# Block kinds from a written table, two more factor sets, and split weights for all columns of the last batch

## The chip, the cores and the metric

The kernel runs on one core of a Trainium2 chip. Its time is the device time of one execution in microseconds (us). Before the change it was 1623.45 us, the median of 4 runs (1623.39 to 1623.63).

The core has five engines with a queue each, worked off in the order in which the program puts instructions there: PE (TensorE, matrix products, with its weight loads shown as PEld), DVE (VectorE), ACT (ScalarE), POOL (GpSimd) and SP (SyncE, which here only issues DMAs). An engine waits at an instruction until the instructions on other engines that it depends on are done.

## What is computed

An attention block with learned inducing points, and then a gated feed-forward block without bias, in 32-bit floats:

```python
def mab(q, kv):
    s = scale * (q @ kv.transpose(0, 2, 1))
    a = softmax(s)                     # written out as max, exp, sum
    return a @ kv
h = mab(I, x)                          # x: 4 batches of 12416 rows, 128 channels; I: 32 rows
x = mab(x, h).reshape(49664, 128)
xn = x / sqrt(mean(x * x) + 1e-6) * rms_g
g = xn @ w_gate                        # 128 -> 1536
out = (silu(g) * (xn @ w_val)) @ w_out # 1536 -> 128
```

The feed-forward block is nearly all of the work: for each row, two products of 128 by 1536 and one of 1536 by 128.

## The kernel before

**Batches, units, blocks.** The four batches are worked off one after the other. The rows of a batch form 25 units: 20 of 512 rows, 4 of 480 and 1 of 256 (line 96). The 1536 hidden columns form NJ = 12 blocks of 128. So a batch has 300 blocks and the whole run 1200; one block of one unit is a *slot* (`slot`, line 674).

**What a slot does.** PE makes the gate product g (line 677) into one of five PSUM banks, ACT takes its SiLU (685), PE makes the value product v (688) into another bank, and DVE multiplies the two (694). The result t, 128 hidden columns by up to 512 rows, must then be multiplied by 128 rows of w_out and added into the unit's accumulator `acc`. There are three ways, the *kinds* of a block:

- *plain*: t goes to SBUF as `u`, and PE multiplies it by the 32-bit `wo` (613 with `acc<-u,wo` in the profile). The profile shows such a product as two records on PE.
- *sums*: t stays in its PSUM bank; ACT makes a rounded, scaled part `hi` of it (659), DVE the remainder `lo` and with it frees the bank (660), and POOL the factor `d` = hi - lo (669).
- *differences*: t goes to SBUF; ACT makes the rounded part (663), POOL the remainder (664), ACT the scaled `hi` (668), and POOL the factor `d` (669).

A block of either of the last two kinds is called *split* here. PE then makes three products in the faster 32-bit type (`F32R`) in place of the plain one: `hi` and `lo` with two parts of the weights into a bank `u3` (633, 635), and `d` with a third part into `acc` (613 with `acc<-xn,more`). When a unit's last split block is through, ACT copies `u3` out (638); `finish` adds it to `acc` (621), transposes and stores.

**Factor sets.** The three factors of a block lie in one of RING = 4 sets, which are taken round-robin from three buffers of `xn` (569 to 571). A set is busy from the first factor until the three products are issued. The three parts of w_out exist for blocks 0 to 9 only (NK = 10, `split_wo`, 566; `weight_of`, 596): blocks 10 and 11 of every unit are plain.

**Stacks.** The weights of g and v differ by batch (they are folded with the inducing rows) and lie in the tiles `sg` and `sv`, two buffers each. Those of the next batch are placed by DMA from its block 199 on (`place`, 459), the tiles being taken at block 193 (`square_h`). Until then the other buffer of each is idle.

**The order.** Attention work for the next batch, and the normalisation (`seam`, 483), is strewn between slots by block number (`schedule`, 823). Which kind a block has, and when PE does the waiting last products, is settled before the program is written, by `rehearse` (929): it runs through all slots with fixed durations for each engine, and records for each slot which products PE does ahead of g, ahead of v and ahead of each step (`picks`). The kind is picked there, slot by slot, by `decide` (1051): sums if that fits, else differences if that fits, else plain. `fits` (1037) adds the candidate's load to eight slots of each engine's load and refuses it where an engine would fall behind PE by more than

```python
LIMIT = (0, 0.8, 0.8, 2.6)   # us: PE, DVE, ACT, POOL (line 926)
```

or by 0.25 us more than it would without. `decide` also refuses blocks near the switches of ACT's table for the exponentials, the first units, and blocks beyond the seventh of the very last unit. Of the 1200 blocks 495 come out plain, 566 sums and 139 differences.

Of the kernel before, what the change touches and what calls it, by code (L numbers as in the profile page):

```python
# [23 lines left out]
def kernel(  # L24
# [74 lines left out]
    NK = NJ - 2  # L99
    RING, RESERVE, HELD, SILU = 4, 7, 9, 3  # L100

    def pool(name, bufs, **kw):
# [463 lines left out]
    def split_wo(step):  # L566

        if not step:
            kws["first"] = xnp.tile([P, half + NK, C], F32R, name=f"xn{full - 1}")
            for name in ("hi", "lo", "d"):  # L570
                kws[name] = xnp.tile([P, RING, 512], F32R, name=f"xn{full - 4 + len(kws) - 2}")

# [9 lines left out]
        for g in range(2):  # L582
# [10 lines left out]
            if at == 6:  # L593
                scaled(0, g, 4096.0)

    def weight_of(kind, j):
        n = kind * NK + j
        return kws["first"][:, n, :] if n < half + NK else kws["more"][:, n - half - NK, :]

    def ffn(b, u):  # L600
# [27 lines left out]

        def project3(j, hi, lo, d):
            if st["k"] == nk:  # L630
                st["u"] = ps_u.tile([P, 512], F32, name="u3")
            ups = st["u"]
            nc.tensor.matmul(ups[:, 0:T], weight_of(0, j), hi, start=st["k"] == nk, stop=False)  # L633
            st["k"] -= 1
            nc.tensor.matmul(ups[:, 0:T], weight_of(1, j), lo, start=False, stop=not st["k"])  # L635
            if not st["k"]:
                o = st["o"] = outp.tile([P, 512], F32, name="o")
                nc.scalar.activation(o[:, 0:T], ups[:, 0:T], AF.Copy, scale=1.0 + 2.0 ** -12)
            project(weight_of(2, j), d)
            kws["out"] -= 1  # L640

# [9 lines left out]
        def three(j, t):  # L651

            assert kws.get("out", 0) < RING
            kws["out"] = kws.get("out", 0) + 1
            n = kws["n"] = (kws.get("n", 0) + 1) % RING
            hi, lo, d = (kws[name][:, n, 0:T] for name in ("hi", "lo", "d"))
            v, kind = t[:, 0:T], kinds[b, u, j]
# [8 lines left out]
            def rest():  # L666
                if kind != "sums":
                    nc.scalar.activation(hi, d.bitcast(F32), AF.Copy, scale=2.0 ** -12)
                nc.gpsimd.tensor_tensor(out=d, in0=hi.bitcast(F32), in1=lo.bitcast(F32), op=ALU.subtract)  # L669
                kara.append(lambda: project3(j, hi, lo, d))  # L670

# [127 lines left out]
    if B > 1:  # L799
        for _ in range(R):  # L800
            load_channels(*pieces[1].pop(0))

    COST = {"turn_x": (0, .63), "scores1": (1.07, .7), "max1": (0, .1), "max2": (.13, .85), "max3": (.1, .1), "turn_e": (0, .63),
            "exp1_of": (0, 0, 1.14), "sum_h": (1.85, .25), "fold_l": (.06, .15), "divide": (0, .6), "turn_h": (.2, .8),
            "square_h": (.1, .76), "stack": (1.1, 1.32), "scores2": (1.07, .63), "row_max": (0, .59), "sub_max": (0, 0, 0, 1.01),
            "exp2": (0, 0, 1.0), "turn_a": (0, .63), "square": (.87,), "turn_z": (0, 1.23), "scale": (0, .7),
            "root": (0, 0, 0, 2.9), "apply": (0, 0, 0, 1.01), "turn_b": (0, .63), "split": (0, 0, .51, 1.25),
            "power": (0, .45), "power_number": (0, 0, .63), "upper": (0, .6), "upper_number": (0, 0, .53), "sign": (0, .6),
            "lower": (0, .6, 0, 1.26), "stack_of": (.87, 0, .5), "stack_low": (0, .62), "split_wo": (0, 0, .7, 1.52)}
    BANKS = {"scores1", "sum_h", "max2", "max3", "fold_l", "turn_h", "square_h", "stack", "scores2", "square", "stack_of"}  # L810
# [3 lines left out]
    TAIL = {"PE": .17, "DVE": .09, "ACT": .11, "POOL": .04}  # L814
    MADE = {"sums": ((-.16,), (0, .6, .49), (0, 0, 0, 1.25)), "differences": ((-.16,), (0, 0, .53, 1.25), (0, 0, .52, 1.25))}
    loads = [[1.29, .6, .5, 0.0] for k in range(B * NU * NJ + 24)]

    def load(k, *costs, sign=1):
        for i, one in enumerate(costs):
            for e, us in enumerate(one):  # L820
                loads[k + i][e] += sign * us

    def schedule(b):
# [4 lines left out]
        def add(k, step, *args):  # L828
            plan.setdefault(int(k), []).append((step, args))
            load(b * NU * NJ + int(k), COST.get(step.__name__, ()))  # L830

        def exponentials(k, step, first):

            groups = list(range(first, NS - 1, 2))
            for i, s in enumerate(groups):
                add(k + i, step, s, NS if s == groups[-1] else s + 2)
                if i:
                    by_tanh.add((b, k + i))
            for at in (k, k + len(groups)):
                load(b * NU * NJ + at, (0, 0, 1.3))  # L840
            return k

        if not b:
# [10 lines left out]
            for s in range(1, NS):  # L854
                add(2 * s + 16, f["scores2"], s)
                add(2 * s + 17, f["row_max"], s)
                add(2 * s + 18, f["sub_max"], s)
            marks.append(exponentials(3 * NS + 9, f["exp2"], 1))
        if b + 1 < B:
            g = attention(b + 1, b + 2 < B)  # L860
# [33 lines left out]
    for k, (b, s) in enumerate(order):  # L894
# [5 lines left out]
        for late_by, one in enumerate(following):  # L900
            for i, step in enumerate(seam(*one)):
# [3 lines left out]
                seams.setdefault(at, []).append((step, ()))  # L905
                load((b * NU + at[1]) * NJ + j, COST.get(step.__name__, ()))
    by_tanh = set()
# [17 lines left out]

    LIMIT = (0, 0.8, 0.8, 2.6)
    kinds, picks = {}, {}

    def rehearse():
# [5 lines left out]
        queues, uses, later, left = {"plain": [], "three": []}, [0], [], {}  # L935
        split = {"out": 0, "u3": 0.0, "all": 0, "made": 0}

# [7 lines left out]
        def soon(k, step):  # L945
            later.append([k, step])

        def has(kind, by):
            if not queues[kind]:
                return False  # L950
            t, unit = queues[kind][0][:2]
            if kind == "three" and not left[unit]["three"]:
                t = max(t, split["u3"])
            return t <= by
# [4 lines left out]
        def issue(kind, to):  # L959
            to.append(kind)  # L960
            t, unit, w = queues[kind].pop(0)[:3]
            split["all"] -= 1
            st = left[unit]
            if kind == "plain":
                end = run("PE", 0.858 * w, t)
            else:
                end = run("PE", 0.697 * w, t)
                split["out"] -= 1
                split["made"] -= 1
                st["three"] += 1  # L970
# [12 lines left out]
        def close(unit, w):  # L983
            st = left[unit]

            def finish():
                run("DVE", 0.6 * w, st["end"], st.get("u3", 0.0))
                soon(1, lambda: run("DVE", 0.63 * w))

# [46 lines left out]

        def fits(k, kind, behind):

            def ahead():
                now = list(behind)  # L1040
                for i in range(k, k + 8):
                    now = [max(0.0, x + one - loads[i][0]) for x, one in zip(now, loads[i])]
                    yield list(now)

            before = list(ahead())
            load(k, *MADE[kind])
            if all(x <= max(most, y + 0.25) for now, old in zip(ahead(), before) for x, y, most in zip(now, old, LIMIT)):
                return True
            load(k, *MADE[kind], sign=-1)

        def decide(b, k, u, j):
            n = b * NU * NJ + k
            if (j >= NK or b == 0 and (u < 2 or k < 26) or (b, u) == flat[-1] and j > 6 or split["out"] > RING or
                    near(b, k, -3, 2)):
                return None
            s = at["PE"]
            behind = [0.0] + [max(0.0, at[e] - s - off) for e, off in (("DVE", 1.2), ("ACT", 0.45), ("POOL", 1.45))]
            return next((kind for kind in ("sums", "differences") if fits(n, kind, behind)), None)

        def slot(b, k, u, j, tanh):  # L1060
            w = per2[units[u][0]] * m / 512.0
            st = left.setdefault((b, u), dict(left=NJ, three=0, open=0, all=False, slots=0, end=0.0))
            kind = decide(b, k, u, j)
            first, second = [], []
# [11 lines left out]
            if kind != "sums":  # L1076
                uses[0] += 1
                while queues["plain"] and queues["plain"][0][3] <= uses[0] - HELD:
                    issue("plain", second)
            while split["made"] == RING and any(one[0] == 1 and one[1].__name__ == "three" for one in later):  # L1080
                issue("three", second)
# [18 lines left out]
            if kind:  # L1100
                kinds[b, u, j] = kind
                split["out"] += 1
                st["open"] += 1

                def three():
                    split["made"] += 1
                    hi = run("ACT", (0.49 if kind == "sums" else 0.53) * w, t)
# [5 lines left out]
                    def rest():  # L1113
                        h = hi if kind == "sums" else run("ACT", 0.52 * w, hi)
                        d = run("POOL", 1.25 * w, lo, h)
                        queues["three"].append((d + 0.05, (b, u), w))

# [20 lines left out]
    for b in range(B):  # L1138
        plan, marks = plans[b]

        unit = {}
        for k, (u, j) in slots(b):

            def steps():
# [54 lines left out]
```

## Time and profile before

| | |
|---|---|
| median of 4 runs | 1623.45 us |
| the profiled execution, its own time | 1623.39 us |
| its span, first to last instruction | 1621.6 us |
| ahead of the first slot's g product | 55.3 us |
| PE busy | 1604.1 us, 99% |
| DVE busy | 1444.5 us, 89% |
| ACT busy | 1238.3 us, 76% |
| POOL busy | 1217.7 us, 75% |

The profile is of one execution. Busy time is the union of an engine's instruction spans. Matmuls are pipelined and their ends are modelled, so that a busy PE is not yet a PE at its peak: what a slot costs PE is better read from the starts of successive products in the timeline. An instruction's span on DVE and ACT is also longer than the distance to the next one's start when they follow without a gap: 128x512 products on DVE last 0.67 us on the mean and start 0.60 us apart; on ACT 0.60 and 0.49; on POOL 1.29 and 1.25.

### The profile page before, as it was taken

The numbers are of one execution on the slowest core, as the hardware profiler recorded it, in microseconds if no ns is written. First come the engines' busy times: TensorE is split into PE (matmuls) and PEld (weight loads), VectorE is DVE, ScalarE is ACT, GpSimd is POOL, SyncE is SP. The second block draws the span as 40 slices with busy tenths as digits, with TensorE's granted clock in tenths as the row PEclk, the third lists the DMA queues.
The fourth block names the chain that finished last, engine by engine and source line by source line (L and its number), as shares of the span: only waits on it lengthen the run. The fifth ranks groups of instructions, "written<-read, shape, count | busy, mean of one in ns | idle before, by whom it ended". The sixth has DMA issues, their size and how long they took to land.

```text
span 1621.6 us, 25435 instructions
## 1 busy us (share of the span) xinstructions
PE 1604.1 (99%) x7085; PEld 1085.1 (67%) x7085; DVE 1444.5 (89%) x2504; ACT 1238.3 (76%) x2285; POOL 1217.7 (75%) x979
## 2 busy tenths in 40 slices
PE   8999999999999999999999999999999999999998
PEld 6546666756676666766677666676667777777776
DVE  4879988999899998899899998789989999999997
ACT  4667877767887778776777777877778888878886
POOL 1358885878588886688678888587858878878876
PEclk9999999999999999999999999999999999999999
DMA  7455624344363141634445323353221122111221
GB/s 262 91 72 85 114 41 100 86 97 69 60 94 59 36 95 29 133 78 79 70 66 83 55 55 67 64 124 79 46 38 29 31 39 40 35 35 36 40 38 26
DMA packets 389181, 112.52 MB, mean 69 GB/s; under 512 B 365072, under 2 KB 369712, under 8 KB 386480
## 3 DMA queue, kind: packets, MB, share of 16 engines
q1 hardware_dynamic: 388304, 110.82, 34.9%
q8 instruction: 56, 0.92, 0.2%
q14 instruction: 85, 0.70, 0.1%
q10 hardware_dynamic: 736, 0.08, 0.0%
HBM read 53.95 MB, written 27.00 MB: 50 GB/s over the span
## 4 chain that ended last, share of the span: by engine, by line
PE 94%; DVE 1%; ACT 1%; issue 1%; POOL 0%; DVEq 0%; ACTq 0%
PE acc L613 35%; PE gv L677 18%; PE gv L688 16%; PE u L635 10%; PE u L633 10%; PE gv L322 3%; PE gv L499 1%; PE gv L378 1%; DVE gv L694 1%; ACT silu L685 1%; PE gv L453 0%; DVE xn L660 0%; PE gv L467 0%; DVE o L621 0%; POOL xn L279 0%
## 5 line engine op out<-in xcount | busy, mean ns | idle before, releaser
L669 POOL TENSOR_TENSOR xn<-xn,xn 128x512 fp32r<-128x512 f32 (+2 forms) x705 | 870.8, 1255 | 268.5 <-DVE xn L660 158.6
L685 ACT ACTIVATE silu<-gv 128x512 f32<-128x512 f32 (+2 forms) x1186 | 689.7, 586 | 258.3 <-PE gv L677 231.5
L688 PE MATMUL gv<-a,sv 128*128 128x512 f32 (+2 forms) x1188 | 636.0, 535 | 0.9 <-ACT silu L685 0.8
L613 PE MATMUL acc<-u,wo 128*128 128x512 f32 (+1 forms) x990 | 490.8, 580 | 0.0
L677 PE MATMUL gv<-a,sg 128*128 128x512 f32 (+2 forms) x1188 | 486.7, 410 | 1.5 <-ACT silu L685 0.8
L694 DVE TENSOR_TENSOR u<-silu,gv 128x512 f32<-128x512 f32 (+2 forms) x621 | 407.6, 663 | 51.7 <-PE gv L688 32.5
L694 DVE TENSOR_TENSOR gv<-silu,gv 128x512 f32<-128x512 f32 (+2 forms) x565 | 376.0, 668 | 66.2 <-PE gv L688 49.0
L660 DVE SCALAR_TENSOR_TENSOR xn<-xn,gv 128x512 fp32r<-128x512 f32 (+2 forms) x566 | 371.2, 656 | 9.5 <-ACT xn L659 5.9
L659 ACT ACTIVATE xn<-gv 128x512 fp32r<-128x512 f32 (+2 forms) x566 | 330.4, 584 | 43.2 <-DVE gv L694 30.9
L677 PEld LDWEIGHTS gv<-a,sg 128*128 128x128 f32 x1188 | 223.7, 188 | 189.4 <-ACT silu L685 40.1
L688 PEld LDWEIGHTS gv<-a,sv 128*128 128x128 f32 x1188 | 223.5, 188 | 139.7 <-issue 45.9
L613 PE MATMUL acc<-xn,more 128*128 128x512 f32 (+2 forms) x705 | 273.5, 388 | 3.0 <-DVE o L621 2.7
L633 PE MATMUL u<-xn,xn 128*128 128x512 f32 (+2 forms) x705 | 272.3, 386 | 0.0
L613 PEld LDWEIGHTS acc<-u,wo 128*128 128x128 f32 x990 | 184.9, 188 | 46.8 <-issue 9.1
L664 POOL TENSOR_TENSOR xn<-u,xn 128x512 fp32r<-128x512 f32 (+2 forms) x139 | 178.6, 1285 | 41.6 <-ACT xn L663 41.6
L635 PE MATMUL u<-xn,xn 128*128 128x512 f32 (+2 forms) x414 | 160.0, 387 | 0.0
L613 PEld LDWEIGHTS acc<-xn,more 128*128 128x128 f32 x705 | 132.3, 188 | 33.5 <-POOL xn L669 5.7
L633 PEld LDWEIGHTS u<-xn,xn 128*128 128x128 f32 x705 | 132.5, 188 | 28.6 <-issue 5.5
L663 ACT ACTIVATE xn<-u 128x512 fp32r<-128x512 f32 (+2 forms) x139 | 87.4, 629 | 36.7 <-DVE u L694 32.4
L635 PE MATMUL u<-xn,more 128*128 128x512 f32 (+2 forms) x291 | 112.5, 387 | 0.0
L516 POOL TENSOR_TENSOR rs<-ms,mhalf 128x16 f32<-128x16 f32 (+2 forms) x28 | 75.9, 2710 | 18.2 <-DVE ms L511 17.2
L635 PEld LDWEIGHTS u<-xn,xn 128*128 128x128 f32 x414 | 77.7, 188 | 17.5 <-DVE gv L694 0.2
(151 smaller groups left out, 1096.4 us busy)
## 6 DMA issues: line engine op xcount, KB each, us to landing
out_dram<-o SPq DMA_DIRECT2D x320, 64.0 KB, 2.0
xT<-in_x_dram SPq DMA_DIRECT2D x60, 256.0 KB, 5.1
xn<-in_x_dram SPq DMA_DIRECT2D x60, 256.0 KB, 4.9
a<-hi SPq DMA_DIRECT2D x156, 64.0 KB, 2.0
a<-lo SPq DMA_DIRECT2D x156, 64.0 KB, 2.0
xn<-in_x_dram SPq DMA_DIRECT2D x5, 1024.0 KB, 10.0
xn<-w SPq DMA_DIRECT2D x18, 256.0 KB, 3.2
out_dram<-o SPq DMA_DIRECT2D x64, 60.0 KB, 2.0
```

Of the source, the lines that this page charges most:

```text
L613: nc.tensor.matmul(acc[:, 0:T], lhsT, rhs, start=st["left"] == NJ, stop=st["left"] == 1)
L633: nc.tensor.matmul(ups[:, 0:T], weight_of(0, j), hi, start=st["k"] == nk, stop=False)
L635: nc.tensor.matmul(ups[:, 0:T], weight_of(1, j), lo, start=False, stop=not st["k"])
L659: nc.scalar.activation(hi, v, AF.Copy, scale=(1.0 - 2.0 ** -13) * 2.0 ** -12)
L660: nc.vector.scalar_tensor_tensor(out=lo, in0=hi.bitcast(F32), scalar=-4096.0, in1=v, op0=ALU.mult, op1=ALU.add)
L663: nc.scalar.activation(d, v, AF.Copy, scale=1.0 - 2.0 ** -13)
L664: nc.gpsimd.tensor_tensor(out=lo, in0=v, in1=d.bitcast(F32), op=ALU.subtract)
L669: nc.gpsimd.tensor_tensor(out=d, in0=hi.bitcast(F32), in1=lo.bitcast(F32), op=ALU.subtract)
L677: nc.tensor.matmul(g[:, 0:T], sg[:, ts(j, P)], a[:, 0:T], start=True, stop=True)
L685: nc.scalar.activation(sl[:, 0:T], g[:, 0:T], AF.Silu)
L688: nc.tensor.matmul(v[:, 0:T], sv[:, ts(j, P)], a[:, 0:T], start=True, stop=True)
L694: nc.vector.tensor_tensor(out=t[:, 0:T], in0=sl[:, 0:T], in1=v[:, 0:T], op=ALU.mult)
```

## The change

- **Kinds from a table.** `decide`, `fits`, LIMIT, MADE and the bookkeeping of loads go. The kinds stand in the program as 900 letters (`s` sums, `d` differences, `.` plain): 300 for batch 0, 300 for batches 1 and 2, 300 for batch 3. `rehearse` still settles the order of the products on PE.
- **Two more factor sets.** The two free buffers of `sg` and `sv` are lent as sets 4 and 5, each with its three factors in thirds of the tile: from block 20 of batch 0 and block 2 of the others. From block 184 they are taken back (`leaving`) except in the last batch, and must be back at block 192. Sets are now taken from a list of idle ones.
- **Split weights for blocks 10 and 11 in the last batch.** `split_last` makes their three parts in the free buffer `xT0` at blocks 2, 4 and 6 of batch 3, with three instructions on ACT and two on POOL of 128x256.
- **In the rehearsal** some PE costs of attention steps are 0.1 to 0.15 us higher, the first product of a unit waits until its bank of `acc` is free (`bank_of`), and the sets are counted as above.

The kinds come out as 411 plain, 561 sums and 228 differences; 34 of the split ones are blocks 10 and 11 of the last batch. In numbers by width, before to after:

| | 512 rows | 480 rows | 256 rows |
|---|---|---|---|
| plain | 393 to 323 | 87 to 78 | 15 to 10 |
| sums | 438 to 446 | 96 to 87 | 32 to 28 |
| differences | 129 to 191 | 9 to 27 | 1 to 10 |

505 of the 1200 blocks change their kind. The number of DMAs is the same.

```diff
+    LENT = (RING, RING + 1)
...
         if not step:
             kws["first"] = xnp.tile([P, half + NK, C], F32R, name=f"xn{full - 1}")
-            for name in ("hi", "lo", "d"):
-                kws[name] = xnp.tile([P, RING, 512], F32R, name=f"xn{full - 4 + len(kws) - 2}")
+            rings = [xnp.tile([P, RING, 512], F32R, name=f"xn{full - 4 + n}") for n in range(3)]
+            kws["sets"] = [[ring[:, n, :] for ring in rings] for n in range(RING)]
+            idle.extend(range(RING))
...
+    def lend(b, k, idle, leaving):
+        if k == (20 if not b else 2):
+            idle += LENT
+            return True
+        if b + 1 < B and k == 184:
+            leaving += [n for n in LENT if n not in idle]
+            idle[:] = [n for n in idle if n not in LENT]
+        assert k != 192 or not leaving
+
+    def give_back(n, idle, leaving):
+        leaving.remove(n) if n in leaving else idle.append(n)
+
+    def lend_tiles():
+        tiles = [stk.tile([P, F], F32R, name=name) for name in ("sg", "sv")]
+        kws["sets"][RING:] = [[t[:, ts(n, 512)] for n in range(3)] for t in tiles]
+
+    def split_last(step):
+        n = NJ - NK
+        if not step:
+            kws["last"] = xtp.tile([P, 3 * n, C], F32R, name="xT0")
+        one, (whi, wlo, ws) = wo[:, NK:NJ, :], (kws["last"][:, ts(kind, n), :] for kind in range(3))
+        if step == 0:
+            nc.scalar.activation(whi, one, AF.Copy, scale=1.0 - 2.0 ** -13)
+            nc.gpsimd.tensor_tensor(out=wlo, in0=one, in1=whi.bitcast(F32), op=ALU.subtract)
+        if step == 1:
+            nc.scalar.activation(wlo, wlo.bitcast(F32), AF.Copy, scale=4096.0)
+            nc.gpsimd.tensor_tensor(out=ws, in0=wlo.bitcast(F32), in1=whi.bitcast(F32), op=ALU.subtract)
+        if step == 2:
+            nc.scalar.activation(whi, whi.bitcast(F32), AF.Copy, scale=4096.0)
+
     def weight_of(kind, j):
+        if j >= NK:
+            return kws["last"][:, kind * (NJ - NK) + j - NK, :]
...
-        def project3(j, hi, lo, d):
+        def project3(j, where):
+            hi, lo, d = (one[:, 0:T] for one in kws["sets"][where])
...
-            kws["out"] -= 1
+            give_back(where, idle, leaving)
...
-            assert kws.get("out", 0) < RING
-            kws["out"] = kws.get("out", 0) + 1
-            n = kws["n"] = (kws.get("n", 0) + 1) % RING
-            hi, lo, d = (kws[name][:, n, 0:T] for name in ("hi", "lo", "d"))
+            where = idle.pop(0)
+            hi, lo, d = (one[:, 0:T] for one in kws["sets"][where])
...
+        if b + 1 == B:
+            for step in range(3):
+                add(2 + 2 * step, split_last, step)
...
-    LIMIT = (0, 0.8, 0.8, 2.6)
+    letters = """
+        ..........................dd...dsd...d....dssd..dssdss.ssd..sdd.sdd.dd...ss.ssd.ss...dsdsdd.s...sssd
...
+        ..sssssss.dsds.s..ssss.ds.sssdds...ssss.ssssssdsss..sdsssd...s..sss.s..dsssdd.ds...dsssssssd.sd.dd..
+    """
+    BLOCKS = [letters[NU * NJ * n:NU * NJ * (n + 1)] for n in (0, 1, 1, 2)]
...
+        def bank_of(unit):
+            older = flat.index(unit) - 2
+            if older < 0 or flat[older] not in left:
+                return 0.0
+            return left[flat[older]].get("turned", 1e9)
...
-            kind = decide(b, k, u, j)
+            kind = {"s": "sums", "d": "differences"}.get(BLOCKS[b][k])
...
-            while split["made"] == RING and any(one[0] == 1 and one[1].__name__ == "three" for one in later):
+            while not idle and any(one[0] == 1 and one[1].__name__ == "three" for one in later):
                 issue("three", second)
```

## The prediction

> **What bounds the kernel now.** I read the page first (shares of busy time, the chain), then PE's timeline for the price of a slot, then the groups by shape, the waits, and busy time by stretch.
>
> ```profile
> span 1621.6 us, 25435 instructions
> ...
> PE 1604.1 (99%) x7085; PEld 1085.1 (67%) x7085; DVE 1444.5 (89%) x2504; ACT 1238.3 (76%) x2285; POOL 1217.7 (75%) x979
> ...
> PEclk9999999999999999999999999999999999999999
> ...
> PE 94%; DVE 1%; ACT 1%; issue 1%; POOL 0%; DVEq 0%; ACTq 0%
> PE acc L613 35%; PE gv L677 18%; PE gv L688 16%; PE u L635 10%; PE u L633 10%; PE gv L322 3%; PE gv L499 1%; PE gv L378 1%; DVE gv L694 1%; ACT silu L685 1%; PE gv L453 0%; DVE xn L660 0%; PE gv L467 0%; DVE o L621 0%; POOL xn L279 0%
> ```
>
> PE bounds it: 94% of the chain that ended last is PE, at a granted clock in the top tenth throughout. Busy PE is partly modelled, so the price of a slot comes from the starts. PE's timeline, columns start and length:
>
> ```profile
> 900.31 0.40 PE L677 MATMUL gv<-a,sg 128*128 128x512 f32 x1
> 900.54 0.39 PE L633 MATMUL u<-xn,xn 128*128 128x512 f32 x1
> 900.77 0.40 PE L635 MATMUL u<-xn,more 128*128 128x512 f32 x1
> 901.01 0.39 PE L613 MATMUL acc<-xn,more 128*128 128x512 f32 x1
> 901.24 0.39 PE L688 MATMUL gv<-a,sv 128*128 128x512 f32 x1
> 901.47 0.39 PE L677 MATMUL gv<-a,sg 128*128 128x512 f32 x1
> 901.70 1.02 PE L613 MATMUL acc<-u,wo 128*128 128x512 f32 x2
> 902.15 0.80 PE L688 MATMUL gv<-a,sv 128*128 128x512 f32 x1
> 902.79 0.39 PE L677 MATMUL gv<-a,sg 128*128 128x512 f32 x1
> ```
>
> From one gate product to the next, the slot with the three products of a split block takes 901.47 - 900.31 = 1.16 us, the one with a plain product 902.79 - 901.47 = 1.32 us. Nothing waits in either. Over the run the medians are 1.160 (498 such slots) and 1.323 (295).
>
> Groups by shape (instructions | busy, mean ns | idle before, what ended it), a wait of PE, and two stretches of 100 us (PE, PEld, DVE, ACT, POOL busy):
>
> ```profile
> L669 POOL TENSOR_TENSOR xn<-xn,xn 128x512 fp32r<-128x512 f32 x567 | 720.7, 1291 | 192.1 <-DVE xn L660 103.5 <-PE gv L677 34.3 <-PE acc L613 18.1
> L664 POOL TENSOR_TENSOR xn<-u,xn 128x512 fp32r<-128x512 f32 x129 | 166.8, 1293 | 41.6 <-ACT xn L663 41.6
> L613 PEld LDWEIGHTS acc<-xn,more 128*128 128x128 f32 x705 | 132.3, 188 | 33.5 <-POOL xn L669 5.7 <-issue 0.5
> ...
> PE acc L613 <- DVE o L621: 2.7, 3, 0.9
> ...
> 1000.00:1100.00 100.00, 99.78 (x538) 67.29 (x537) 84.35 (x146) 76.57 (x138) 70.58 (x54) 1.00 0.37 81
> 1300.00:1400.00 100.00, 99.89 (x381) 71.27 (x380) 91.94 (x150) 79.13 (x146) 82.21 (x63) 1.00 0.18 34
> ```
>
> A split block costs POOL 1.29 us (sums) or 2.58 us (differences). PE's last product of it has waited for POOL's factor only 5.7 us in the whole run. POOL's share differs by stage, 71% to 82% here, and PE is no idler where it is higher.
>
> **The change, part by part.**
>
> *Kinds.* 84 more blocks are split (plain 495 to 411; 70 of 512 rows, 9 of 480, 5 of 256). At 512 rows each saves PE 1.323 - 1.160 = 0.163 us. At 480 the tail of the timeline has 1.09 (1581.38 to 1582.47) against 1.24 (1584.66 to 1585.90): 0.15. At 256 no pure plain slot stands; half of the 512 price, 0.08, is an estimate. 70 x 0.163 + 9 x 0.15 + 5 x 0.08 = 11.4 + 1.4 + 0.4 = **13.2 us off PE**, the engine on the path. The two blocks 10 and 11 per unit of the last batch are 34 of these 84.
>
> *What pays for it.* Sums go down by 5, differences up by 89. POOL gets 89 more remainders and 84 more factors: by width 132 x 1.291 + 27 x 1.22 + 14 x 0.738 = 214 us. ACT gets 8 x 0.60 - 9 x 0.57 - 4 x 0.38 for sums and 62 x 1.26 + 18 x 1.20 + 9 x 0.80 for differences: 105 us. DVE loses 2 us. Shares become POOL 1432/1610 = 89%, ACT 1343/1610 = 83%, DVE 90%. None of it lies on PE; the cover is PE's own 1.16 us or more per slot, and it holds as long as no engine is past it for longer than the factor sets bridge.
>
> *By stage.* I took each stretch of 50 blocks of the run before, and added the change of kinds at the distances between starts (POOL 1.25 us, ACT 0.49 to 0.54, DVE 0.60). Batch 2, blocks 200 to 249 (1121.5 to 1192.7): plain 18 to 13, differences 5 to 9, sums 27 to 28; POOL 58.8 + 9 x 1.25 = 70.1 of 71.2 - 0.8 = 70.4 us, 99%; DVE 94%, ACT 79%. The highest shares of POOL that come out: 99% there in the first three batches, 95% at blocks 150 to 199, and in the last batch 98%, 96% and 100% at blocks 100 to 249 in a row. Before, no such stretch has POOL above 88%. So POOL is filled nearly to PE's time, and not over it.
>
> *How far POOL falls behind in between.* A running sum, block by block, of POOL's work (the two instructions, and the attention steps) less the slot's PE time, never below zero: before, the mean is 0.6 us and the peak 2.9; after, the mean is 2.0 and the peaks 4 to 6, with 8.6 once, at blocks 100 to 125 of batch 0. This is the wait that can take the place of the saving: PE's order is fixed, so behind a product whose `d` is late stand all later g and v, and behind them SiLU and DVE. The bounds: the 5.7 us that PE waited for `d` may grow with the mean backlog, 2.0/0.6 = 3.3 times, to 19 (+13); or this wait and that for the bank of `acc` (2.7 us, which the rehearsal now counts) vanish: -8.4. Six sets bridge some six slots, 7 us, four sets 4.6 us; all peaks but two or three lie under that, and the row nearest to the new state, the stretch from 1300, shows no idle PE at POOL 82%. I take -1, the `acc` wait partly gone.
>
> *DVE beside a busier POOL.* By the trace's instructions, the DVE multiply of a slot (128x512) takes 681 ns where POOL works beside it for over 95% of its length (593 of them) and 683 ns where it hardly does (84): no price. The Trainium skill, "SBUF — State Buffer", section "Who interferes with whom", says that DVE and GpSimd share one port pair under an exclusive lock, on which the second one blocks. Read as holding for every instruction it speaks against this change: 214 us more of POOL would push DVE, at 89%, past PE. The same section frees a DVE instruction with at most one SBUF input outside the two-port modes; the slot's multiplies read one operand from PSUM, and the two durations agree. By the first reading the sum would end far slower, by the second it stays as it is.
>
> *Lent sets.* Their first writer in a batch waits for the last g and v of the batch before, done two blocks earlier. Taken back late they would hold up `place`, whose stacks are needed some 100 slots later: hidden by over 100 us. Their DMAs and those queued behind on SP are the same in number. Priced at 0; without that cover it is the length of the delay, a few us per batch.
>
> *`split_last`.* Three ACT instructions of 0.38 and two POOL of 0.74 (the rows of 256 columns), 2.6 us, off PE, at blocks where POOL's share comes to 90%. First needed at block 11: 0.
>
> *The end.* Before, PE's last products are plain; after, three split blocks stand last, two of the three differences, so POOL's chain sets the end. In the last unit POOL gets some 6.3 us for blocks 3 to 9 (at 0.70), PE has about 5.6: at worst +3, and -2 if the 2.0 us which PE loses there now (0.6, 1.1, 0.3 at slots 293, 294, 296) go. I take +1, nearer to the new chain.
>
> **Sum.** -13.2 - 1 + 1 = -13.2 against the profiled 1623.39 us (span 1621.6 and 1.8 around it, 0.06 below the median): 1610.2. As the term for late factors is one-sided in risk, I round up to **1611 us**.
>
> **The rivals.**
>
> *A. It gives nearly all back (same, 1616 to 1627).* Late `d`s cost PE up to the +13 worked out above: 1610.2 + 14 = 1624. For it: the backlog is three times as long. Against: extra sets, and an order on PE that was laid out for these kinds.
>
> *B. POOL becomes the bound (slower).* The place is blocks 200 to 249 of the first three batches and 100 to 249 of the last. If POOL can in practice be kept busy for no more than a share c of a stretch, each stretch lasts its POOL work divided by c. Over all stretches this adds 10 us at c = 0.96, 15 at 0.95, 22 at 0.94, 39 at 0.92. It decides from c = 0.955 down: at 0.94 the time is 1610 + 22 = 1632, at 0.92 1649. For it: 0.88 is the most that the run before shows, and each POOL instruction waits for others. Against: within runs POOL goes without gaps (four factors in 5.04 us at 988.73), at a spread of 1.248 median to 1.259 for nine in ten.
>
> *C. It gives more.* Waits of 0.15 to 0.6 us in some 30 slots before sum to about 10 us; kinds chosen over a whole run may avoid them too: 1600 to 1606. Against: shares that high leave less play.
>
> *D. The change doesn't do what it says:* the lent sets stay unused or the letters don't take. The built program's instruction list excludes it: 411 plain, and `sg`, `sv` as factors.
>
> **How the numbers follow.** Forecast (1606 to 1616) 0.52; C (below 1606) 0.18; A 0.17, of which 0.07 below 1620.2 and 0.10 within 0.2%; B 0.13. A measurement of this kernel tells about 0.2%, 3.2 us, from no change: faster means below 1620.2, slower above 1626.7. Faster 0.52 + 0.18 + 0.07 = 0.77, same 0.10, slower 0.13. The range leaves out B, the upper part of A and the lowest part of C (some 0.04): 1601 to 1622.
>
> **What would show it.** In the profile after: 323 plain products of 512 rows (646 records); the slots' 1.16 and 1.32 us unchanged; POOL near 89%; the multiply on DVE still near 0.68 us; PE's waits for POOL's factor at 5 to 10 us in all. A figure over 15 there, with the highest 50-block stretches longer than before, is A or B. Wrong, too, if POOL's instructions grow longer, or if the end after the last g takes over 3 us more than now.

## The result, and the profile after

The changed kernel takes **1621.32 us** (median of 42 runs, 1620.37 to 1622.21), the kernel before 1623.04 us on the same chips (60 runs, 1622.21 to 1623.84). The ratio is 0.9989, with a 95% interval of 0.9984 to 0.9993: a gain of 1.7 us, a tenth of a per cent, where 12.4 were forecast. The profiled execution took 1621.94 us.

The page of the kernel after, beginning with its span, then the busy time of each engine, the granted clock, and the shares of the chain that ended last:

```profile
span 1620.0 us, 26069 instructions
...
PE 1594.7 (98%) x7169; PEld 1098.7 (68%) x7169; DVE 1454.6 (90%) x2499; ACT 1304.4 (81%) x2461; POOL 1427.0 (88%) x1154
...
PEclk9999999999999999999999999999999999999999
...
PE 86%; ACT 3%; DVE 3%; issue 2%; POOL 2%; DMA 1%; SPq 1%; POOLq 0%; DVEq 0%; ACTq 0%
```

The shares of the loads came out near the forecast: POOL 88%, ACT 81%, DVE 90%. But DVE, which was to lose 2 us of work, is busy 10.1 us more (1444.5 to 1454.6). PE is busy 9.4 us less, yet the span is only 1.6 us shorter, and PE's share of the chain has dropped from 94% to 86%: other engines now hold it up here and there. The same two stretches of 100 us as before (PE, PEld, DVE, ACT, POOL busy):

```profile
1000.00:1100.00 100.00, 99.27 (x550) 69.11 (x549) 87.42 (x150) 83.04 (x153) 92.30 (x71) 1.00 0.38 82
1300.00:1400.00 100.00, 99.39 (x391) 72.30 (x390) 95.80 (x156) 84.75 (x159) 94.32 (x74) 1.00 0.17 32
```

PE is short of full by 0.73 and 0.61 us in 100, against 0.22 and 0.11 before; DVE went up by 3 to 4 points in both. Which waits these are, PE's waits say (us in total, times, longest):

```profile
PE gv L716 <- ACT silu L724: 4.4, 8, 1.0
PE gv L716 <- DVE u L733: 3.3, 6, 1.5
PE gv L727 <- DVE u L733: 2.4, 5, 1.2
...
PE acc L653 <- POOL xn L708: 0.4, 1, 0.4
```

At its products PE waits for POOL's factor hardly at all. It waits with the next g or v, because DVE's product (`u`) or ACT's SiLU, which free a PSUM bank, are late. Before, the two waits for `u` were not in the list, and the one for SiLU at the g product was

```profile
PE gv L677 <- ACT silu L685: 1.3, 2, 0.8
```

**Where the span went.** I fitted one price per kind of PE instruction to the distances between starts in both traces where nothing waits, summed them over all PE instructions from the first g product to the last to get *PE's work*, and call what the distances have above it *stall*. The fit is an estimate; the slots' medians, 1.160 and 1.323 us, are the same in both traces.

| us | before | after | change | forecast |
|---|---|---|---|---|
| ahead of the first g | 55.3 | 54.9 | -0.4 | 0 |
| PE's work | 1513.1 | 1499.7 | -13.4 | -13.2 |
| stall | 45.8 | 55.7 | +9.9 | -1 |
| after the last g product | 7.3 | 9.7 | +2.4 | +1 |
| span | 1621.6 | 1620.0 | -1.6 | -13.2 |

So the saving is there in full, and 12.3 us of it are given back. By stretches of 100 blocks the stall grew in the first three batches nearly everywhere, by up to 4.3 us at blocks 200 to 299 of batch 0 (4.25 to 8.56), and fell at the end of the last (3.79 to 1.67).

**What is late on DVE.** Groups of DVE by shape (instructions | busy, mean ns | idle before). In the kernel before, the scaling of the sums of squares in `scale`:

```profile
L511 DVE TENSOR_SCALAR ms<-ms 128x16 f32<-128x16 f32 x20 | 6.4, 318 | 0.7
L511 DVE TENSOR_SCALAR ms<-ms 128x15 f32<-128x15 f32 x4 | 2.3, 573 | 0.1
L511 DVE TENSOR_SCALAR ms<-ms 32x8 f32<-32x8 f32 x4 | 0.6, 158 | 0.1
```

In the kernel after:

```profile
L512 DVE TENSOR_SCALAR ms<-ms 128x16 f32<-128x16 f32 x20 | 15.8, 792 | 0.7
L512 DVE TENSOR_SCALAR ms<-ms 32x8 f32<-32x8 f32 x4 | 2.4, 606 | 0.1
L512 DVE TENSOR_SCALAR ms<-ms 128x15 f32<-128x15 f32 x4 | 2.2, 540 | 0.1
```

The same instruction on the same 16 numbers per partition has become 2.5 times as long. Over its three shapes and 28 instructions it took 9.3 us of DVE before and takes 20.4 us after. The timeline shows what it is waiting out (start, length, idle before in brackets):

```profile
112.65 0.67 DVE L511 TENSOR_REDUCE ms<-z 128x16 f32<-128x512 f32 x1
113.01 1.27 POOL L708 TENSOR_TENSOR sg<-sg 128x512 fp32r<-128x512 f32 x1
...
113.35 0.96 DVE L512 TENSOR_SCALAR ms<-ms 128x16 f32<-128x16 f32 x1
114.23 1.27 DVE L733 TENSOR_TENSOR u<-silu,gv 128x512 f32<-128x512 f32 x2
114.39 2.91 POOL L517 TENSOR_TENSOR rs<-ms,mhalf 128x16 f32<-128x16 f32 x1
114.96 0.50 PE L716 MATMUL gv<-a,sg 128*128 128x512 f32 x1 [1.45 <-DVE u L733]
```

POOL's factor runs to 113.01 + 1.27 = 114.28, the scaling to 113.35 + 0.96 = 114.31. The products behind it on DVE start late, their banks come free late, and PE stands 1.45 us. This is the rule of all of them: in the two traces together 36 of the 56 scalings have a POOL instruction in progress at their start (9 of 28 before, 27 of 28 after), and each of the 36 ends 20 to 36 ns after an instruction of POOL ends. For 34 it is the one that was in progress, and the scaling takes at most 1.17 us; two, of 1.31 and 2.02 us, end only with POOL's next instruction. The other 20 take 158 to 176 ns.

### The profile page after: what moved, and what is told of

Its sections match the earlier page's. It is cut to its first block, busy times and chain, and to the rows that moved or that the text cites. A ratio compares the mean times of both kernels' runs of the same rounds, so it can differ in the third digit from the quotient of the medians.

```text
span 1620.0 us, 26069 instructions
## 1 busy us (share of the span) xinstructions
PE 1594.7 (98%) x7169; PEld 1098.7 (68%) x7169; DVE 1454.6 (90%) x2499; ACT 1304.4 (81%) x2461; POOL 1427.0 (88%) x1154
## 4 chain that ended last, share of the span: by engine, by line
PE 86%; ACT 3%; DVE 3%; issue 2%; POOL 2%; DMA 1%; SPq 1%; POOLq 0%; DVEq 0%; ACTq 0%
PE acc L653 29%; PE gv L716 17%; PE gv L727 15%; PE u L676 10%; PE u L674 10%; PE gv L323 2%; PE gv L379 1%; PE gv L500 1%; ACT silu L724 1%; DVE u L733 1%; POOL xn L708 1%; ACT sc L440 0%; ACT xn L698 0%; DVE gv L733 0%; DVE xn L699 0%
## 5 line engine op out<-in xcount | busy, mean ns | idle before, releaser
L708 POOL TENSOR_TENSOR xn<-xn,xn 128x512 fp32r<-128x512 f32 (+2 forms) x605 | 746.2, 1252 | 78.3 <-DVE xn L699 34.4
L653 PE MATMUL acc<-u,wo 128*128 128x512 f32 (+2 forms) x822 | 409.7, 581 | 0.6 <-DVE u L733 0.6
L698 ACT ACTIVATE xn<-gv 128x512 fp32r<-128x512 f32 (+2 forms) x433 | 252.5, 583 | 65.8 <-DVE gv L733 53.5
L699 DVE SCALAR_TENSOR_TENSOR xn<-xn,gv 128x512 fp32r<-128x512 f32 (+2 forms) x433 | 283.7, 655 | 12.7 <-ACT xn L698 7.0
L703 POOL TENSOR_TENSOR xn<-u,xn 128x512 fp32r<-128x512 f32 (+2 forms) x172 | 217.4, 1264 | 13.2 <-ACT xn L702 13.2
L674 PE MATMUL u<-xn,xn 128*128 128x512 f32 (+2 forms) x581 | 228.7, 394 | 0.0
L653 PE MATMUL acc<-xn,more 128*128 128x512 f32 (+2 forms) x581 | 224.5, 386 | 0.6 <-POOL xn L708 0.4
L708 POOL TENSOR_TENSOR sv<-sv 128x512 fp32r<-128x512 f32 (+2 forms) x92 | 117.8, 1280 | 10.2 <-DVE sv L699 5.6
L674 PEld LDWEIGHTS u<-xn,xn 128*128 128x128 f32 x581 | 109.3, 188 | 25.1 <-issue 5.6
L708 POOL TENSOR_TENSOR sg<-sg 128x512 fp32r<-128x512 f32 (+1 forms) x92 | 118.1, 1284 | 7.0 <-PE u L676 2.0
L676 PE MATMUL u<-xn,xn 128*128 128x512 f32 (+2 forms) x288 | 110.7, 384 | 0.0
```

Source lines behind the costliest of these rows:

```text
L653: nc.tensor.matmul(acc[:, 0:T], lhsT, rhs, start=st["left"] == NJ, stop=st["left"] == 1)
L698: nc.scalar.activation(hi, v, AF.Copy, scale=(1.0 - 2.0 ** -13) * 2.0 ** -12)
L699: nc.vector.scalar_tensor_tensor(out=lo, in0=hi.bitcast(F32), scalar=-4096.0, in1=v, op0=ALU.mult, op1=ALU.add)
L703: nc.gpsimd.tensor_tensor(out=lo, in0=v, in1=d.bitcast(F32), op=ALU.subtract)
```

## The experiments

The theory (P): these scalings, made longer by a busier POOL, are the main part of what is given back. Rivals: the table's kinds are bad as such for the order on PE; the raised prices or the wait for a bank of `acc` in the rehearsal are bad; the last unit's letters; the lent sets. Each time is a median with the kernel before's on the same chip beside it; runs beside the same value of it share a chip.

### Does the scaling cost it?

In e1 the kernel after gets the scaling in a form that also writes an accumulator, the lower clamp left out:

```diff
-nc.vector.tensor_scalar(out=ms, in0=ms, scalar1=1.0 / C, scalar2=1e-6, op0=ALU.mult, op1=ALU.max)
+spare = small.tile([P, 1], F32, name="tiny")[rows, :]
+nc.vector.tensor_scalar(out=ms, in0=ms, scalar1=1.0 / C, scalar2=None, op0=ALU.mult, op1=ALU.max,
+                        accum_out=spare)
```

> The changed kernel, with one DVE instruction in another form: the scaling of the sums of squares by 1/C (128x16, SBUF to SBUF, 28 times) is written with an accumulator output; the clamp at 1e-6 is left out. Theory P (shared port): that instruction went from a mean of 318 ns before to 792 ns after, because it waits out the POOL instruction in progress, and the delays on a DVE that is at 90% hold up PSUM banks and so PE. In the new form it does not take the pair of ports: its mean falls below 350 ns, the waits of PE shrink by 4 to 8 of the 9.9 us by which they grew, 1613 to 1617 us. Theory T (tight table): the table of kinds leaves DVE and ACT no play at all, and small delays of every sort now reach PE; the instruction may get shorter, but the time moves by 0 to 2 us only, 1619 to 1621.

Measured: **1613.27 us** (1612.33 to 1613.68) against 1623.39, ratio 0.9936 (0.9922 to 0.9951): 8.0 us below the kernel after, at the lower end of the 1613 to 1617 that P expected and far from T's 1619 to 1621. DVE's group in e1, and the same place of the timeline:

```profile
L513 DVE TENSOR_SCALAR_CACHE_REDUCE ms<-ms 128x16 f32<-128x16 f32 x20 | 3.4, 170 | 0.7
...
L513 DVE DVE_READ_ACCUMULATOR ms<-ms 128x1 f32 x24 | 2.0, 83 | 0.0
```

```profile
113.22 1.28 POOL L710 TENSOR_TENSOR sg<-sg 128x512 fp32r<-128x512 f32 x1
113.56 0.17 DVE L513 TENSOR_SCALAR_CACHE_REDUCE ms<-ms 128x16 f32<-128x16 f32 x1
113.65 0.08 DVE L513 DVE_READ_ACCUMULATOR ms<-ms 128x1 f32 x1
113.65 1.28 DVE L735 TENSOR_TENSOR u<-silu,gv 128x512 f32<-128x512 f32 x2
114.39 0.50 PE L718 MATMUL gv<-a,sg 128*128 128x512 f32 x1 [0.67 <-DVE u L735]
```

POOL's factor runs from 113.22 to 114.50, and the scaling beside it takes 0.17 us. PE's stall is 47.1 us, 8.6 less than after, a little more than the 4 to 8 expected, at the same kinds and the same order of work on PE.

In e2 the same edit is made to the kernel before, where only 9 scalings meet a POOL instruction.

> The kernel before with the same other form of that DVE instruction (the clamp at 1e-6 left out). Theory P: POOL is 75% busy here and the instruction at 318 ns, so at most 28 x 0.2 us of DVE are won: 1621.5 to 1623. Theory T: the same. A gain as large as in the changed kernel would say that the form is simply cheaper, and has nothing to do with the change.

Measured: 1622.37 us, ratio 0.9995 (0.9985 to 1.0004). By itself the accumulator form gains 1.0 us here, which can't be told from nothing; the 8 us come only in the kernel with the busier POOL.

That leaves open whether the time goes with DVE being held, or with `ms` itself coming late to `root`, POOL's instruction that reads it. e11 keeps e1's scaling and adds to `turn_b`, a later DVE step of the same seam, 28 times, an instruction of the old kind whose result has the same value and which nobody is waiting for:

```diff
 def turn_b():
+    nc.vector.tensor_scalar(out=ident[:, 0:16], in0=ident[:, 0:16], scalar1=1.0, scalar2=0.0, op0=ALU.mult, op1=ALU.add)
     aT = st["aT"] = work.tile([P, 512], F32, name="aT", tag="work")
```

> The changed kernel with the accumulator form (1613.3 us), and one more DVE instruction in each of the 28 seams: 16 columns of the constant identity times 1 plus 0, SBUF to SBUF in the plain form, ahead of the split. Theory P: it waits out POOL's instruction like the scaling did (mean near 0.65 us with POOL busy) and costs PE 4 to 9 us: 1617 to 1622. Rival: only its own length counts, 28 x 0.17 us of DVE: 1613.5 to 1615.5.

Measured: 1620.33 us against 1623.05, ratio 0.9984 (0.9974 to 0.9993): 7.1 us above e1. Its row:

```profile
L528 DVE TENSOR_SCALAR ident<-ident 128x16 f32<-128x16 f32 x28 | 16.8, 599 | 0.0
```

DVE being held is enough. Without the wait the 28 would have taken some 28 x 0.17 = 4.8 us of DVE's time; they took 16.8.

### The end

e3 is the kernel after with the last unit's twelve letters as before; e6 has this and e1's scaling.

```diff
-        ..sssssss.dsds.s..ssss.ds.sssdds...ssss.ssssssdsss..sdsssd...s..sss.s..dsssdd.ds...dsssssssd.sd.dd..
+        ..sssssss.dsds.s..ssss.ds.sssdds...ssss.ssssssdsss..sdsssd...s..sss.s..dsssdd.ds...dsssssssssd......
```

> The changed kernel with the kinds of the last unit's 12 blocks as they were before (splits up to the seventh block, six plain ones last; in the changed kernel two of the last three splits are differences). From the last g product to the end the changed kernel takes 9.7 us, the one before 7.3. Theory E (the end's chain on POOL): this goes back to 7.2 to 7.8 us, the time to 1619 to 1620. Rival: what the end wins is lost in slots 288 to 299 as stalls of 0.3 to 1.1 us as before, and the time stays within 0.5 us of 1621.3.

> The changed kernel with both repairs: the scaling of the sums of squares in the form with an accumulator (its clamp left out), and the last unit's kinds as before. If the two are separate causes they add up: 1613.3 - 1.3 = 1612.0, within 0.5. If the end's gain came only because that unit was held up by late DVE work, it is gone here: 1613.0 to 1613.5.

Measured: e3 1620.02 us (1619.35 to 1620.91), ratio 0.9979 (0.9969 to 0.9988); e6 **1611.41 us** (1611.12 to 1611.88) against 1623.30, ratio 0.9927 (0.9913 to 0.9942). The letters cost 1.3 us in one pair and 1.9 in the other, and the two edits add up. After the last g there are 8.7 us in place of 9.7, so 1.4 of the 2.4 stay: expected was all of it back. For the sum of the two edits 1612.0 was expected, within 0.5; it came out 0.1 below that. The last rows of the kernel after (start, length) show the part that went:

```profile
1612.57 0.73 POOL L708 TENSOR_TENSOR sv<-sv 128x256 fp32r<-128x256 f32 x1
1613.26 0.74 POOL L703 TENSOR_TENSOR xn<-u,xn 128x256 fp32r<-128x256 f32 x1
1614.05 0.38 PE L676 MATMUL u<-xn,more 128*128 128x256 f32 x1 [0.19 <-POOL xn L703]
1614.08 0.72 POOL L708 TENSOR_TENSOR xn<-xn,xn 128x256 fp32r<-128x256 f32 x1
1614.85 0.38 PE L653 MATMUL acc<-xn,more 128*128 128x256 f32 x1 [0.42 <-POOL xn L708]
1615.33 0.42 DVE L661 TENSOR_TENSOR o<-acc,o 128x256 f32<-128x256 f32 x1 [3.08 <-PE acc L653]
```

Three POOL instructions stand one behind the other, and PE's last two products wait for them. In e6 the last step is set by `u3`'s copy on ACT:

```profile
1604.26 0.19 PEld L655 LDWEIGHTS acc<-sg,more 128*128 128x128 f32 x1
1604.37 0.28 PE L655 MATMUL acc<-sg,more 128*128 128x256 f32 x1
1604.57 0.38 ACT L681 ACTIVATE o<-u 128x256 f32<-128x256 f32 x1 [2.92 <-PE u L678]
1604.99 0.42 DVE L663 TENSOR_TENSOR o<-acc,o 128x256 f32<-128x256 f32 x1 [2.31 <-ACT o L681]
```

The traces also say what the other 1.4 us are. Behind the last g product's start PE does six plain products and the products of two split blocks in e6, and four and one in the kernel before; its last product ends 3.69 us after that start in e6 and 2.49 before, 1.2 us later. The copy of `u3` behind it makes up the rest. So most of the 1.4 us is work that stands behind the last g product in place of ahead of it, not time lost.

### Are the kinds or the rehearsal to blame?

e4 is the kernel after with all 1200 letters as the kernel before picked them; e5 has the table but the old prices in the rehearsal; e7 has both.

```diff
-            "exp1_of": (0, 0, 1.14), "sum_h": (2.0, .25), "fold_l": (.16, .15), "divide": (0, .6), "turn_h": (.3, .8),
...
+            "exp1_of": (0, 0, 1.14), "sum_h": (1.85, .25), "fold_l": (.06, .15), "divide": (0, .6), "turn_h": (.2, .8),
...
```

> The changed kernel, but with the kinds of all 1200 blocks as the rule of the kernel before picked them (495 plain, 566 sums, 139 differences): lent sets, the split weights and the changed rehearsal stay. Theories P and T both put saving and give-back into the kinds: PE's work is as before, POOL's share 75%, the time 1621 to 1624. If it comes out above 1626, the lent sets or the new order of products cost by themselves, and the give-back is theirs.

> The changed kernel with the PE costs of attention steps in the rehearsal as they were before the change (kinds, lent sets, bank_of and split weights stay). With the old kinds the new rehearsal cost 8 us. Theory C (raised costs): they lay the waiting products in places where they hold up the chip, with any table; without them the time falls by 3 to 8 us, 1613 to 1618. Theory K (the order must fit its kinds): the table was found with the raised costs, and any other order of products with it is worse: 1621 to 1628.

> The kinds of the kernel before with the old PE costs in the rehearsal; lent sets, bank_of and split weights of the changed kernel stay. Theory C: the 7.8 us that the old kinds lost in the new frame come from the raised costs, and the time is back at 1622.5 to 1624.5. Theory S (lent sets and the wait for the bank of acc in the rehearsal): it stays at 1629 to 1632.

Measured: e4 1631.18 us against 1623.39, ratio 1.0047 (1.003 to 1.0063), outside what was expected; e5 1622.27 against 1623.30, ratio 0.9993 (0.9984 to 1.0003); e7 1629.62, ratio 1.0039 (1.0024 to 1.0054). The old kinds under the new rehearsal lose 8 us, so the table is worth 10 us there, more than the 1.7 that the whole change shows. The raised prices are not what is given back: without them the table's kernel is no faster (0.9993 of the kernel before, against 0.9989 with them; the intervals overlap). And they are not what ails e4, since e7 is only 1.6 us better.

Two parts of the change remain that could ail the old kinds: the lent sets, and the wait for a bank of `acc` (`bank_of`). e9 and e10 take one of them each from e4.

```diff
-    LENT = (RING, RING + 1)
+    LENT = ()
```

```diff
         def bank_of(unit):
...
-            return left[flat[older]].get("turned", 1e9)
+            return 0.0
```

> The kinds of the kernel before in the changed kernel without the two lent sets; the bank_of wait and the raised costs of the rehearsal stay. In the frame with lent sets the old kinds cost 6 to 8 us. Theory S1 (with six sets the rehearsal puts off split products, and DVE and ACT work bunches): without them the time is back at 1623 to 1625. Theory S2 (the bank_of wait moves the products): it stays at 1629 to 1632.

> The kinds of the kernel before in the changed kernel with lent sets, but the rehearsal does not wait for the bank of acc (bank_of gives 0). Theory S2: back at 1623 to 1625. Theory S1: it stays at 1629 to 1632.

Measured: e9 1630.82 us against 1623.05, ratio 1.0048 (1.0033 to 1.0063); e10 1624.42, ratio 1.0009 (0.9999 to 1.0018). It is the wait for the bank: with the old kinds it costs 6.8 us, and the rest of the change beside the kinds nothing that can be told from 0.2%. Does it cost the table's kinds as much? e13 takes it from the kernel after.

> The changed kernel, the rehearsal without the wait for the bank of acc (bank_of gives 0), the table and all else as it is. With the old kinds that wait in the rehearsal cost 6.8 us (1631.2 with it, 1624.4 without). Theory W (it puts the first product of a unit off with any table, and the products behind it bunch): 1615 to 1619. Theory K (the table was chosen with it, and holds only with the order that it gives): 1621 to 1630.

Measured: 1619.90 us (1619.31 to 1620.59) against 1622.93, ratio 0.9981 (0.9972 to 0.999): 1.3 to 1.4 us, between the two expectations. So it is a small part with the table.

### The lent sets, and the same rule elsewhere on DVE

e8 takes the lent sets from the kernel after (the edit of e9, with the table).

> The changed kernel without the two lent sets: the table of kinds runs with four factor sets, and the rehearsal issues a split block's products early where no set is idle. Theory B (backlog of POOL): the six sets carry the longer backlog, and with four PE waits for POOL's factors at many places: 1628 to 1645, with the waits for POOL in the list of PE's waits. If the sets were not needed: 1620 to 1624.

Measured: 1645.59 us against 1623.30, ratio 1.0136 (1.012 to 1.0153), just above what was expected. PE's weight loads in e8, and its waits:

```profile
L653 PEld LDWEIGHTS acc<-xn,more 128*128 128x128 f32 x755 | 141.8, 188 | 41.8 <-POOL xn L708 12.3
```

```profile
PE gv L716 <- ACT silu L724: 6.2, 13, 1.0
PE acc L653 <- POOL xn L708: 4.1, 9, 0.8
PE u L676 <- POOL xn L703: 2.1, 2, 1.1
```

This is what late factors look like, the wait that I had feared: 12.3 us at the loads and 4.1 at the products, and a stall of 79.9 us. In the kernel after the row reads

```profile
L653 PEld LDWEIGHTS acc<-xn,more 128*128 128x128 f32 x581 | 109.1, 188 | 25.9 <-POOL xn L708 3.9
```

and the rows of the lent sets add 0.5 us. The two more sets are worth 24 us to the table, and keep it ahead of the kernel before at all.

e12 gives the accumulator form also to the division of `hn` and the product `hg`, whose means had gone from 696 to 869 and from 518 to 683 ns (four each); e14 has this and e13's edit.

```diff
-nc.vector.tensor_scalar_mul(out=hg[:], in0=st["hT"][:], scalar1=gam)
+nc.vector.tensor_scalar(out=hg[:], in0=st["hT"][:], scalar1=gam, scalar2=None, op0=ALU.mult, op1=ALU.max,
+                        accum_out=spare[:])
```

> The changed kernel with both repairs (1611.4 us), and the two other scalings from SBUF to SBUF in the attention part (the division of h and its product with the norm weight, 8 instructions at 0.68 to 0.87 us) in the accumulator form too. Theory P: each gets shorter by 0.3 to 0.5 us; with 8 of them the time falls by 0 to 1.5 us, 1610 to 1611.5. If it rises, the accumulator's extra read costs more than the wait.

> The best kernel so far (accumulator form for the three scalings, the last unit's kinds as before; 1610.8 us), the rehearsal without the wait for the bank of acc. Theory W: 1604 to 1609. Theory K: 1611 to 1620.

Measured: e12 1610.80 us, ratio 0.9925 (0.991 to 0.994), 12.25 us below its kernel before where e6 was 11.9 below: not to be told apart. e14 **1609.99 us** (1609.68 to 1610.09) against 1622.93, ratio 0.9921 (0.9904 to 0.9938): the fastest of all, 12.9 us below the kernel before, and between its two expectations.

## Why the prediction was wrong

**PE's work: right.** 70, 9 and 5 blocks at the prices of the slots gave -13.2 us; the fit over both traces gives -13.4, at unchanged prices of 1.160 and 1.323.

**The loads and POOL: right for POOL, too high for ACT.** POOL was to get 214 us and got 209; it stands at 88% against 89%, and its factor takes 1.297 us against 1.291. ACT was to get 105 us and got 66 (81% against 83%): its spans added up grew by 108, but spans overlap where instructions follow without a gap, and busy time counts such overlap once. POOL can be kept this busy: in the trace after it is at 97 or 98% in four of the 24 stretches of 50 blocks, so rival B is out.

**Lent sets and `split_last`: right.** Both were priced at 0, and neither shows up in PE's waits as a cost. e8 shows how much cover the sets give.

**The late factors: the mechanism was wrong.** The term of -1 with bounds of -8.4 to +13 was about PE waiting for `d`. At the weight loads that wait went from 5.7 us to 4.4 (3.9 and 0.5), and at the products 0.4 are new. Yet PE's stall grew by 9.9, by a way that the term did not see: a late DVE. The time fell into rival A's range, but not by A's mechanism.

**"DVE beside a busier POOL: no price" is the step that failed.** I measured it on one instruction, the slot's multiply, which reads one operand from PSUM. For it the answer holds (681 ns before, 679 after). Then I took it for all of DVE. The Trainium skill, "SBUF — State Buffer", section "Who interferes with whom", which I had read for or against the change as a whole, distinguishes by instruction: it counts `tensor_scalar` among the forms that can enter the two-port modes and so contend, when their operands meet the conditions, and leaves out the form that also writes out its accumulator. The runs agree with both halves: 28 scalings with input and output in SBUF went from 9.3 to 20.4 us, and in the accumulator form 27 of them beside a POOL instruction took 148 to 171 ns (e1). The trace before had it all: a mean of 318 ns for an instruction that is 0.17 us where POOL rests, 9 of 28 prolonged. A split of that row by what POOL was doing, as I did for the multiply, would have given the price: a POOL at 88% leaves few scalings unhit, and each hit one loses about the rest of a factor, half of 1.29 us. With the 27 hits against 9 that the traces show this estimate is 18 x 0.65 = 12 us more on an engine at 90% of its time. Measured: 11.1 us more on DVE, and 8.0 us on the run (e1).

**The end: the sign was right, the size not.** +1 was taken and +2.4 measured, inside the +3 of the worst case. e3 gives 1.0 of it back at the last rows; the other 1.4 are mostly products that stand behind the last g in place of ahead of it. The reading of the letters was off too: all three split blocks that stand last are differences, not two of them. The sum of 6.3 us for POOL counts them rightly.

**Where the 12.3 us given back went.** About 8 to the scalings (e1), 1.3 to 1.9 to the last unit's letters (e3, e6), 0.8 to 1.4 to the wait for a bank in the rehearsal (e14 against e12, e13). That makes 10.1 to 11.3; 1 to 2 us are open. A candidate that no run tests: other small DVE instructions from SBUF to SBUF grew as well and were left as they were, the four subtractions `sc<-sc,mx` from 683 to 1018 ns and the four `row<-row` from 274 to 508 ns, 2.3 us of DVE together. The rehearsal cannot see the largest part: it prices reduction and scaling together at 0.7 us of DVE (`"scale": (0, .7)`), where the two now take 0.67 and 0.79 us on the mean (128x512 and 128x16), and the scaling's length depends on POOL. For the table the rehearsal had PE's idle time fall by 5.6 us; on the chip the stall rose by 9.9.

**Open.** Why the wait for a bank costs the greedy rule's kinds 6.8 us and the table's little over 1 is not shown. In e4 PE waits 4.6 us with v for SiLU where e10 has 0.8, and the 2.5 us that it waits for the bank in e10 are gone in e4; how the one leads to the other was not followed. That the table fits an order made with that wait is an argument only.

## What to carry to other kernels

When a change fills an engine further, look at every instruction of its neighbours that may share a resource with it, above all the small ones that both read and write SBUF, and split each row's durations by what the other engine does at that moment: one kind that goes undisturbed says nothing of the next. A short instruction with a mean of twice its shortest is the sign (here 318 against 158 ns). Where a plan of fixed durations chooses how full an engine gets, first make those durations independent of it (here the accumulator form, 8.0 us), and then choose.

## What was not expected of the hardware

- A DVE instruction on 128x16 numbers, 158 to 176 ns by itself, took up to 1.17 us by waiting for POOL's instruction in progress, and in two cases, 1.31 and 2.02 us, for the next one too; the end follows the end of a POOL instruction by 20 to 36 ns in all 36 cases.
- The scaling with an accumulator output (and without the clamp) is free of it, 148 to 171 ns beside POOL, at the price of one more instruction of 83 ns.
- A DVE instruction that nobody waits for cost the run 7.1 us in 28 pieces of 0.60 us (e11), with DVE at 90% and five banks between PE and DVE: here slack on average was no cover.
